# Two-layer MoE behind a Fourier mix on one core: layer two without POOL arithmetic, with later accumulations and earlier side sums

## The chip, the cores and the metric

One core of one Trainium2 chip. The metric is device microseconds of one execution, the median of several runs. Times on the trace start at the span's first instruction.

## What is computed

`x` is 2 x 3008 x 256 in float32. A Fourier transform runs over sequence and feature axis, its real part goes through two feed-forward layers of width 2048:

```python
X = np.fft.fft(np.fft.fft(x, axis=1), axis=2).real.astype(np.float32).reshape(6016, 256)
h = X @ w_in                                            # layer one
X = (np.maximum(h, 0) + alpha * np.minimum(h, 0)) @ w_out
h = X @ moe2_w_in                                       # layer two
out = (h * (1.0 / (1.0 + np.exp(-h)))) @ moe2_w_out
```

## The kernel before

The symmetry of the transform leaves half of the tokens. They are cut into six **chunks** (c = 0 to 5) of up to 512 columns. Every float32 product is done as three TensorE passes, high x high, low x high and high x low, where `high` is a rounded copy (ScalarE, ACT) and `low` is the remainder (a subtraction on VectorE, DVE, or on POOL).

**Layer one** runs in 96 steps (16 per chunk): three plus three passes into a bank, the leaky step on DVE and ACT, `gh` (ACT, L726) and `gl` (POOL, L727), then twelve passes into `pso` (L742). Into these steps the program slips side work by tables of step numbers: the Fourier stages of later chunks, the narrowing of the 64-bit weights, and for layer two `factors` (L835, L836, L840: splits of x into high and low) and `x2_sums` (L785: four subtractions per chunk, on POOL, whose result is stored to DRAM as `xf` by L789 on SP's queue).

**Layer two** works on **pairs** of 128 hidden rows, eight per chunk (p = 0 to 7). It is a fast matrix product with seven products instead of eight. Chunk 0 is done the plain way: per pair seven steps of one trio (L883, three passes) with pieces of the pair before's second product (L977) between them; two of its four lows are POOL's (`ghl`, L904). Chunks 1 to 5 follow the lists `SEQ`: one string per kind of pair, whose tokens are issued in that order. M1 to M7 are trios of the first product (L883); O1 to O7 are groups of three passes of the second (L1078), a pair late (`-1`); 7 + 7 times three is 42 passes a pair. u and m copy a bank (ACT), c adds a bank (DVE, L1090), s is the silu (ACT, L1098), T a difference of two results (L1091), h a high (ACT, L1092), l a low (L1091), E a sum on DVE. A token that ends in `g` has its subtraction on POOL instead of DVE. `sequence(c, p)` picks the string: A, B, C for the first three pairs of chunks 2 to 5, F0 to F2 for chunk 1, N in the middle, L at the end, K5 and L5 for the last two pairs of all.

Three things run beside that in chunks 1 to 4 and 2 to 5:

- **Factors of the next chunk** (`fh`, `fl`, one of each in pairs 1 to 7). `make_high` copies the high out of `raw32` into one of three spare tiles (`tail[c, "spare"][i % 3]`) and sends the previous factor to DRAM (`fdr`, L1029, SP). `make_low` writes minus the rounded value (L1037) and has POOL issue a DMA that adds the exact x onto it (L1038).
- **Ends of the chunk before** (`ending`): copies of the accumulators (L1137), then accumulations a1 to a5 as POOL DMAs into the output tile `ob` (L1129), by the table `DRAIN` behind M7 of a pair: a1, a3 in pair 2, a2 in pair 3, a4 and a5 in pair 4. a4 adds `o[:, 0, 1]` onto `o[:, 1, 1]`, and a5 then writes `o[:, 0, 1]`. Each finished quarter is written out by `write` (L1122, SP).
- **SP's queue** carries `sring` (weights of the second product), `sides` (raw32), `fdr`, the quarters of the output and, in chunk 0, the weights `y<-stash_o` and `y<-stash_i` that narrowing had put by.

POOL, SP, ACT and DVE each take their instructions in the program's order: a waiting one holds all behind it.

Of the kernel before, what the change touches and what calls it, by code (L numbers as in the profile page):

```python
# [14 lines left out]
ALU = mybir.AluOpType  # L15
# [14 lines left out]
BUFS = {"h": 2, "r": 2, "gh": 3, "gl": 2, "pb": 2, "raw": 2, "y": 2}  # L30
# [67 lines left out]
def kernel(  # L98
# [110 lines left out]
    def place_raw():  # L209
        while started and held[3] == BUFS["raw"]:  # L210
            yield EARLY
        held[3] += 1
# [55 lines left out]
    stage_s = {}  # L268

    def mixed_wout(n, y):  # L270

        a = [[y[:, m, k * P:(k + 1) * P] for k in range(2)] for m in range(2)]
        while True:
            c = now[0] // NF
            if now[0] % NF < NF - 3:
                if c not in stage_s:
                    t = spot(f"px{c - 1}", [2, 4, 2, P], F32R, "stage_s")
                    stage_s[c] = [t[:, i] for i in range(2)]
                if stage_s[c]:
                    break  # L280
            yield EARLY
        w = stage_s[c].pop(0)
        s = f32(w)[:, :, 1]
        yield AMID
        G.tensor_tensor(s[:, 0], a[0][1], a[1][1], op=ALU.add)
        G.tensor_tensor(s[:, 1], s[:, 0], a[0][0], op=ALU.subtract)
        yield EARLY
        yield AMID
        G.tensor_tensor(s[:, 2], a[0][0], a[0][1], op=ALU.subtract)
        G.tensor_tensor(s[:, 3], a[1][0], s[:, 1], op=ALU.subtract)  # L290
        active.append([store_s(n, c, w, s), EARLY])

    def store_s(n, c, w, s):
# [8 lines left out]
        stage_s[c].append(w)  # L302
# [504 lines left out]
    def slot(n):  # L807

        if n not in slots:
            if n < 4 or n > 7:  # L810
                t = spot({0: "px4", 2: "wo1_0", 8: "px3"}[n], [2, 2, 512], F32R, "ts")
# [8 lines left out]
    def place(c, j):  # L820
        return (7 * (c - 1) + 5 + j) % 8 if c else (0, 1, 2, 3, 8, 9, 4)[j]
# [200 lines left out]
    def make_high(c, i):  # L1022
        u = MAKE[i]
        t = made[c, u] = tail[c, "spare"][i % 3]
        A.activation(t[0], raw32[(7 * c + i) % 2], AF.Copy)
        while unsaved:
            v = unsaved.pop()
            for a in range(2):
                nc.sync.dma_start(fdr[v][:, a], f32(made[v][a]))  # L1029

    unsaved = []

    def make_low(c, i):
        u = MAKE[i]
        lo = made[c, u][1]
        g, s, k = SOURCE[TURN[u]]
        A.activation(lo, raw32[(7 * c + i) % 2], AF.Copy, scale=-1.0)  # L1037
        G.dma_start(f32(lo), xf[c][g][:, s, k], accum_op=ALU.add)  # L1038
        if i + 2 < 7:
            load_raw32(c, i + 2)  # L1040
        if 2 <= u < 6:
            unsaved.append((c, u))
        else:
            factor[c, TURN[u]] = made[c, u]
            split2.add((c, TURN[u]))
# [34 lines left out]
    def token(n, name, other):  # L1080
# [26 lines left out]
        elif name == "E":  # L1107
# [4 lines left out]
            else:  # L1112
                add(outbuf(c)[:, 0, 0], tail["acc"], accum[c, "O1"])
                write(c, 0, 0)
# [43 lines left out]
    def perform(n, name, other):  # L1158
# [34 lines left out]
    def start_win2():  # L1193
# [35 lines left out]
    }  # L1229
    DRAIN = {2: "a1 a3", 3: "a2", 4: "a4 a5"}  # L1230
# [29 lines left out]
    with tc.manual_schedule():  # L1260
# [181 lines left out]
        def sequence(c, p):  # L1442
# [4 lines left out]
            return "ABCNNNNL"[p] if c > 1 else "NNNNNNNL"[p]  # L1447
# [9 lines left out]
        for n, (c, p) in enumerate(pairs):  # L1457
# [110 lines left out]
```

## Time and profile before

| what | us |
|---|---|
| median of three runs (lowest, highest) | 955.98 (955.15, 958.06) |
| profiled execution | 955.43 |
| its span, first to last instruction | 953.6 |

The page gives busy time per engine; the trace gives each instruction's start, duration and, in brackets, the engine's idle time before it and what ended that. A row of the timeline may stand for several instructions (`x3`). A window's row gives the busy time of each engine in that stretch, the granted TensorE clock (1.00 is 2.4 GHz, 0.50 is 1.2 GHz) and the DMA engines' share.

### The profile page before, as it was taken

To read this page: it belongs to the slowest core of one execution; us is meant where nothing else is said; L and a number is where in the kernel's file an instruction comes from. 1 tells how busy PE (TensorE), PEld (TensorE's weight loads), DVE (VectorE), ACT (ScalarE), POOL (GpSimd) and SP (SyncE) were. 2 spreads that over 40 slices of the span, in tenths; PEclk is the share of its full clock that TensorE was granted. 3 is DMA by queue.
4 is the path that set the end of the run, shared out by engine and by line. 5 is a ranking of instruction groups with operands and counts; after the bars stand their busy time and mean duration, and the time that the engine had idled before them with its cause. 6 is when DMAs were issued, how large, how long until landed. Compare 5 with 4: busy or idle time off the path is not lost.

```text
span 953.6 us, 12772 instructions
## 1 busy us (share of the span) xinstructions
PE 923.8 (97%) x4237; PEld 767.5 (80%) x4237; DVE 757.8 (79%) x1130; ACT 697.3 (73%) x1247; POOL 529.8 (56%) x390
## 2 busy tenths in 40 slices
PE   9999999999999999999999999999899999999997
PEld 8899888888788787788897878877778778777875
DVE  4877755676787699766665689998899798899998
ACT  5787666666675576666665788898799789788775
POOL 0498868585786688999897642223223213313121
PEclk9999999999999999999999999999999999999999
DMA  9411123134333450112212267539566863964421
GB/s 340 146 45 51 48 56 75 50 86 158 132 133 126 125 169 22 48 64 78 82 51 84 73 161 198 173 103 232 154 178 160 226 178 98 243 172 130 109 78 66
DMA packets 58477, 116.83 MB, mean 123 GB/s; under 512 B 7238, under 2 KB 14508, under 8 KB 57260
## 3 DMA queue, kind: packets, MB, share of 16 engines
q1 hardware_dynamic: 50780, 102.35, 33.7%
q0 software_dynamic: 6912, 12.59, 7.8%
q10 hardware_dynamic: 720, 1.10, 0.3%
q8 instruction: 33, 0.54, 0.2%
q14 instruction: 32, 0.26, 0.1%
HBM read 77.32 MB, written 33.44 MB: 116 GB/s over the span
## 4 chain that ended last, share of the span: by engine, by line
PE 68%; issue 10%; POOL 9%; DVE 6%; DMA 4%; ACT 2%; SPq 0%; POOLq 0%; ACTq 0%; DVEq 0%
PE pso L742 21%; PE psh L883 16%; PE psh L651 11%; PE psm L1078 10%; PE pso L977 3%; POOL gl L727 2%; PE psE L1078 2%; PE psB L466 1%; DVE ghl L1091 1%; PE psW L602 1%; POOL ob L1129 1%; DVE ring L1090 1%; DVE ring L1091 1%; PE psU L1322 1%; POOL forms L1091 1%
## 5 line engine op out<-in xcount | busy, mean ns | idle before, releaser
L727 POOL TENSOR_TENSOR gl<-r,gh 128x1024 fp32r<-128x1024 f32 (+1 forms) x96 | 227.2, 2368 | 59.2 <-ACT gh L726 37.1
L883 PE MATMUL psh<-ts,wi 128*128 128x512 f32 (+1 forms) x864 | 229.8, 389 | 5.3 <-DVE ring L1090 3.1
L883 PEld LDWEIGHTS psh<-ts,wi 128*128 128x128 f32 x864 | 161.9, 189 | 41.3 <-DVE ring L1090 6.0
L742 PE MATMUL pso<-gh,wo_o 128*128 128x512 f32 (+1 forms) x768 | 191.6, 387 | 0.5 <-ACT x L759 0.5
L742 PEld LDWEIGHTS pso<-gh,wo_o 128*128 128x128 f32 x768 | 143.9, 188 | 28.3 <-ACT x L759 0.9
L651 PE MATMUL psh<-pq,wa 128*128 128x512 f32 (+1 forms) x576 | 148.5, 391 | 3.4 <-DVE h L671 3.1
L1091 DVE TENSOR_TENSOR ghl<-ring,ghl 128x512 fp32r<-128x512 f32 x185 | 139.8, 770 | 8.7 <-ACT ghl L1092 8.7
L1092 ACT ACTIVATE ghl<-ring 128x512 fp32r<-128x512 f32 x200 | 122.5, 624 | 30.2 <-DVE ring L1091 13.5
L700 DVE SCALAR_TENSOR_TENSOR psd<-h,psh 128x512 f32<-128x512 f32 (+1 forms) x96 | 65.6, 683 | 88.5 <-PE psh L651 87.8
L651 PEld LDWEIGHTS psh<-pq,wa 128*128 128x128 f32 x576 | 106.5, 188 | 26.2 <-DVE h L671 5.1
L726 ACT ACTIVATE gh<-r 128x1024 fp32r<-128x1024 f32 (+1 forms) x96 | 99.9, 1040 | 35.2 <-DVE r L711 32.9
L1091 DVE TENSOR_TENSOR ring<-ring 128x512 f32<-128x512 f32 x153 | 111.0, 726 | 13.7 <-POOL forms L1091 9.4
L701 ACT ACTIVATE r<-psh 128x512 f32<-128x512 f32 (+1 forms) x96 | 56.5, 588 | 74.4 <-DVE psd L700 58.4
L742 PE MATMUL pso<-gl,wo_o 128*128 128x512 f32 (+1 forms) x384 | 101.7, 386 | 0.1
L1078 PE MATMUL psm<-ghl,sring 128*128 128x512 f32 x360 | 96.1, 391 | 1.2 <-DVE ghl L1091 1.2
L1090 DVE TENSOR_TENSOR ring<-ring,psh 128x512 f32<-128x512 f32 x120 | 81.7, 681 | 9.9 <-ACT ring L1092 5.0
L1092 ACT ACTIVATE ring<-psh 128x512 f32<-128x512 f32 x120 | 70.7, 589 | 18.2 <-PE psh L883 18.0
L742 PEld LDWEIGHTS pso<-gl,wo_o 128*128 128x128 f32 x384 | 71.9, 188 | 14.5 <-POOL gl L727 1.1
L1098 ACT ACTIVATE ring<-ring 128x512 f32<-128x512 f32 x120 | 74.5, 624 | 11.1 <-DVE ring L1090 10.9
L711 DVE SCALAR_TENSOR_TENSOR r<-r,al,psh 128x512 f32<-128x512 f32 (+1 forms) x96 | 70.7, 736 | 14.9 <-ACT r L701 13.4
L1078 PEld LDWEIGHTS psm<-ghl,sring 128*128 128x128 f32 x360 | 67.5, 188 | 17.1 <-DVE ghl L1091 2.8
L1038 POOL DMA_DIRECT2D ts<-xf x21 | 19.4, 926 | 106.8 <-ACT ts L1037 98.4
(148 smaller groups left out, 1524.7 us busy)
## 6 DMA issues: line engine op xcount, KB each, us to landing
sring<-sdr SPq DMA_DIRECT2D x40, 512.0 KB, 4.1
raw<-in_w_in SPq DMA_DIRECT2D x16, 512.0 KB, 6.4
raw<-in_w_out SPq DMA_DIRECT2D x16, 512.0 KB, 3.6
xf<-x SPq DMA_DIRECT2D x8, 1024.0 KB
sides<-xf SPq DMA_DIRECT2D x28, 256.0 KB, 4.7
ts<-fdr SPq DMA_DIRECT2D x26, 256.0 KB, 5.5
fdr<-ts SPq DMA_DIRECT2D x24, 256.0 KB, 4.6
ts<-xf POOLq DMA_DIRECT2D x21, 256.0 KB, 5.8
```

What stands on the lines that cost most here:

```text
L651: T.matmul(bank[:, :w], wa[q][:, mm, eo, a, :], pq[c][:, 2 * eo + bb, :w], start=eo == 0 and a == bb, stop=bb == 1, skip_group_check=True)
L700: V.scalar_tensor_tensor(other[:, :w], t[:, :w], 2.0, bank[:, :w], op0=ALU.mult, op1=ALU.subtract)
L711: V.scalar_tensor_tensor(r[:, s, :w], r[:, s, :w], al[:, m:m + 1], h[:, :w], op0=ALU.mult, op1=ALU.add)
L726: A.activation(hi[:, :, :w], r[:, :, :w], AF.Copy)
L727: G.tensor_tensor(lo[:, :, :w], r[:, :, :w], f32(hi[:, :, :w]), op=ALU.subtract)
L742: T.matmul(po[c][s][k][:, :w], wo1[q][:, mm, a, k * P:(k + 1) * P], g[:, s, :w], start=m == 0 and a == 0 and g is hi, stop=m == NF - 1 and ...
L883: T.matmul(dst[:, :w], wi2[p][:, FORMS[j], a], t[:, :w], start=start and a == 0 and t is hi, stop=t is lo, skip_group_check=True)
L1078: T.matmul(dst, w, form[f][:, g], start=first and b == g == 0, stop=last and g == 1, skip_group_check=True)
L1090: add = lambda dst, a, b: V.tensor_tensor(dst, a, b, op=ALU.add)
L1091: sub = lambda dst, a, b: eng.tensor_tensor(dst, a, b, op=ALU.subtract)
L1092: copy = lambda dst, src: A.activation(dst, src, AF.Copy)
L1098: A.activation(side_of[f], x if f == "21" else side_of[f], AF.Silu)
```

## The change

- The lists of `SEQ` are new (C is dropped; the third pair is an N). None of the strings of chunks 1 to 4 has a `g` token; K5 and L5 leave three subtractions to POOL.
- `DRAIN` puts a4 into pair 4 and a5 into pair 5. Chunks before the last write their four quarters together, behind M7 of pair 6 (`LAST`).
- `make` replaces `make_high` and `make_low`; in most strings the low comes first, and a factor is stored when the high of the factor two later is made.
- `raw` has three buffers and there is a tile `more` (8 KB a partition). It holds `stage_s` in layer one and two factor slots in chunk 0; chunk 1's factors get slots of their own, all but one.
- The step tables `SUMS`, `AGAIN` and `T1` are earlier: chunk 2's sums by 16 to 19 steps, chunk 3's by 8 to 17, chunk 4's (reloaded by `again`) by 17 to 20, chunk 5's by 20 to 26, chunk 1's factors by 4 to 15.

The diff, with one of the new strings:

```diff
-BUFS = {"h": 2, "r": 2, "gh": 3, "gl": 2, "pb": 2, "raw": 2, "y": 2}
+BUFS = {"h": 2, "r": 2, "gh": 3, "gl": 2, "pb": 2, "raw": 3, "y": 2}
...
-                    t = spot(f"px{c - 1}", [2, 4, 2, P], F32R, "stage_s")
+                t = spot("more", [2, 4, 2, P], F32R, "stage_s")
...
-                t = spot({0: "px4", 2: "wo1_0", 8: "px3"}[n], [2, 2, 512], F32R, "ts")
+                t = spot({0: "px4", 2: "wo1_0", 8: "px3", 10: "more"}[n], [2, 2, 512], F32R, "ts")
...
-        return (7 * (c - 1) + 5 + j) % 8 if c else (0, 1, 2, 3, 8, 9, 4)[j]
+        return ((0, 1, 2, 3, 8, 9, 4), (5, 6, 12, 7, 10, 11, 0))[c][j]
...
+    def make(c, i, low):
+        u = MAKE[i]
+        if (c, u) not in made:
+            made[c, u] = tail[c, "spare"][i % 3]
+        hi, lo = made[c, u]
+        raw = raw32[(7 * c + i) % 2]
+        if low:
+            g, s, k = SOURCE[TURN[u]]
+            A.activation(lo, raw, AF.Copy, scale=-1.0)
+            G.dma_start(f32(lo), xf[c][g][:, s, k], accum_op=ALU.add)
+        else:
+            A.activation(hi, raw, AF.Copy)
+            if i > 1 and 2 <= MAKE[i - 2] < 6:
+                for a in range(2):
+                    nc.sync.dma_start(fdr[c, MAKE[i - 2]][:, a], f32(made[c, MAKE[i - 2]][a]))
+        if (c, u, not low) in halfway:
+            if i + 2 < 7:
+                load_raw32(c, i + 2)
...
-            write(c, 1, 0)
+            write(c, 1, 0, c == NC - 1)
...
-        "N": ("M1 s22-1 h21-1 E-2 s12-1 M2 h22-1 O1-1 m1 fh l21-1 M6 T1-1 l22-1 O3-1 hT1-1 c11 T3-1 M5 fl lT1-1 "
-               "u2 hT3-1 M7 s11 O5-1 u3 T2-1 lT3-1 T4-1 O7-1 M4 hT2-1 c22 M3 h11 hT4-1 s21 lT2-1 lT4-1 c12 O6-1 "
-               "O2-1 O4-1 l11g "),
+        "N": ("M1 s12-1 h21-1 O3-1 E-2 T1-1 m1 l21-1 fl hT1-1 M2 M6 T3-1 O1-1 c11 M5 hT3-1 T2-1 lT1-1 u2 M7 "
+               "hT2-1 lT3-1 O5-1 s11 u3 T4-1 c22 h11 lT2-1 hT4-1 s22 O7-1 M4 M3 O6-1 s21 O2-1 h22 lT4-1 l11 O4-1 "
+               "c12 fh l22 "),
...
-    DRAIN = {2: "a1 a3", 3: "a2", 4: "a4 a5"}
+    DRAIN = {2: "a1 a3", 3: "a2", 4: "a4", 5: "a5"}
+    LAST = 6
...
-    SUMS = {2: (69, 72, 75, 78), 3: (81, 86, 88, 89), 5: (126, 132, 134, 139)}
-    AGAIN = 111, 4, (115, 118, 120, 124)
-    T1 = 40, 42, 46, 47, 48, 49, 50, 51, 53, 54, 55
+    SUMS = {2: (50, 56, 57, 60), 3: (66, 69, 78, 81), 5: (106, 108, 111, 113)}
+    AGAIN = 90, 4, (96, 98, 103, 105)
+    T1 = 28, 30, 31, 33, 36, 38, 43, 44, 47, 49, 51
...
+                    if p == LAST:
+                        for i in range(4):
+                            write(c - 1, i // 2, i % 2)
```

Three places show how the instructions stand. First POOL in pairs 2 to 6 of chunk 2; `ts<-xf` is a factor's low, `ob<-` are the accumulations, `forms` the low of a result that PE needs. Before:

```order
L1038 DMA ts<-xf_1_69 128x512 x2
L1129 DMA ob<-ob 128x512
L1091 TENSOR_TENSOR forms<-ring,forms 128x512
L1038 DMA ts<-xf_1_69 128x512
L1129 DMA ob<-ob 128x512
L1129 DMA ob<-t_98 128x512
L1091 TENSOR_TENSOR forms<-ring,forms 128x512
L1038 DMA ts<-xf_0_68 128x512
```

and after:

```order
L1030 DMA ts<-xf_1_69 128x512
L1129 DMA ob<-ob 128x512
L1030 DMA ts<-xf_1_69 128x512
L1129 DMA ob<-ob 128x512
L1030 DMA ts<-xf_0_68 128x512
L1129 DMA ob<-t_98 128x512
L1030 DMA ts<-xf_0_68 128x512 x2
```

The `forms` rows are gone from POOL, and `ob<-t_98` (a5) no longer stands right behind the accumulation whose source it overwrites (a4).

Second, POOL in pairs 0 to 2 of chunk 0; `ghl` are the lows of chunk 0's results, `wi` and `wAo` weights, `x` the side sums. Before:

```order
L904 TENSOR_TENSOR ghl<-ring,ghl 128x448
L382 TENSOR_TENSOR wi_5_4420<-t_98,wi_5_4420 128x4x128
L904 TENSOR_TENSOR ghl<-ring,ghl 128x448
L324 TENSOR_TENSOR wAo_4170<-y_4500,wAo_4170 128x2x256
L324 TENSOR_TENSOR wAo_4529<-y_4502,wAo_4529 128x2x256
L904 TENSOR_TENSOR ghl<-ring,ghl 128x448
```

and after:

```order
L902 TENSOR_TENSOR ghl<-ring,ghl 128x448
L783 TENSOR_TENSOR x_4147<-x_4147 128x512
L380 TENSOR_TENSOR wi_5_4422<-t_98,wi_5_4422 128x4x128
L783 TENSOR_TENSOR x_4147<-x_4147 128x512
L783 TENSOR_TENSOR x_4445<-x_4445 128x512
L902 TENSOR_TENSOR ghl<-ring,ghl 128x448
L783 TENSOR_TENSOR x_4445<-x_4445 128x512
L322 TENSOR_TENSOR wAo_4171<-y_4505,wAo_4171 128x2x256
L322 TENSOR_TENSOR wAo_4536<-y_4507,wAo_4536 128x2x256
L902 TENSOR_TENSOR ghl<-ring,ghl 128x448
```

Four side sums now stand between the lows of pair 0's end and pair 1's end.

Third, SP in pairs 4 to 6 of chunk 2. Before:

```order
L1020 DMA sides<-xf_0_68 128x512
L1122 DMA out_dram<-ob 128x512
L1014 DMA sring<-sdr_2818 128x1024
L1029 DMA fdr_4_80<-ts 128x512 x2
L1020 DMA sides<-xf_0_68 128x512
L1122 DMA out_dram<-ob 128x512 x2
L1014 DMA sring<-sdr_3061 128x1024
L1029 DMA fdr_5_81<-ts 128x512 x2
```

and after:

```order
L1012 DMA sring<-sdr_3064 128x1024
L1035 DMA fdr_4_80<-ts 128x512 x2
L1018 DMA sides<-xf_0_68 128x512
L1012 DMA sring<-sdr_3209 128x1024
L1122 DMA out_dram<-ob 128x512 x4
L1035 DMA fdr_5_81<-ts 128x512 x2
```

The stores of factors and the loads no longer stand behind single quarters of the output; the last store of a factor stands behind all four.

## Rows read from the trace of the kernel before

**Rows 1.** The page, part 1: engine, busy us, share of the span, instructions.

```profile
PE 923.8 (97%) x4237; PEld 767.5 (80%) x4237; DVE 757.8 (79%) x1130; ACT 697.3 (73%) x1247; POOL 529.8 (56%) x390
```

**Rows 2.** Windows by chunk of layer two: length, busy (instructions) by engine, clock, DMA.

```profile
459.50:536.50 77.00, 74.67 (x361) 67.45 (x360) 50.56 (x74) 47.95 (x91) 65.72 (x60) 1.00 0.26 88
536.50:617.10 80.60, 77.46 (x340) 63.09 (x339) 71.26 (x104) 69.29 (x132) 26.48 (x23) 1.00 0.56 151
617.10:699.50 82.40, 78.79 (x338) 63.85 (x337) 72.89 (x113) 69.90 (x132) 22.95 (x22) 0.98 0.66 176
699.50:781.00 81.50, 78.75 (x337) 63.81 (x336) 72.82 (x113) 69.67 (x132) 22.86 (x22) 0.98 0.66 177
781.00:862.10 81.10, 78.03 (x337) 62.48 (x337) 73.26 (x113) 69.71 (x133) 22.92 (x22) 1.00 0.66 179
862.10:953.60 91.50, 84.01 (x358) 65.94 (x356) 84.22 (x127) 68.84 (x127) 22.11 (x18) 0.99 0.32 86
```

**Rows 3.** Timeline of PE: start, us; the first trio of pairs 3 to 6, chunk 2.

```profile
646.44 0.84 PE L883 MATMUL psh<-spare,wi 128*128 128x512 f32 x3
...
655.96 0.84 PE L883 MATMUL psh<-spare,wi 128*128 128x512 f32 x3
...
666.41 0.84 PE L883 MATMUL psh<-spare,wi 128*128 128x512 f32 x3
...
680.34 0.84 PE L883 MATMUL psh<-spare,wi 128*128 128x512 f32 x3
```

**Rows 4.** Waits of PE, whole span: us in total, times, longest.

```profile
PE psm L1078 <- POOL forms L1091: 5.9, 3, 2.5
```

**Rows 5.** Timeline around the longest of these waits: POOL and PE.

```profile
661.16 1.20 POOL L1129 DMA_DIRECT2D ob<-ob  x1
...
668.70 0.87 POOL L1129 DMA_DIRECT2D ob<-t  x1 [6.34 <-PE psm L1078]
...
670.92 0.64 PE L1078 MATMUL psm<-forms,wAo 128*128 128x512 f32 x1 [2.54 <-POOL forms L1091]
```

**Rows 6.** Windows: the stretch after that wait, columns as in rows 2.

```profile
671.10:674.50 3.40, 3.40 (x9) 2.62 (x10) 3.40 (x6) 2.77 (x5) 0.88 (x1) 0.50 0.65 139
```

**Rows 7.** Timeline, pair 4 of chunk 2: ACT and PE.

```profile
658.61 0.63 ACT L1025 ACTIVATE ts<-sides 128x512 fp32r<-128x512 f32 x1 [1.14 <-DMA fdr<-ts]
...
660.81 0.97 PE L883 MATMUL psh<-ts,wi 128*128 128x512 f32 x3 [0.61 <-ACT ring L1092]
```

**Rows 8.** Timeline, pair 0 of chunk 3: DVE beside POOL and alone.

```profile
699.51 1.59 POOL L1091 TENSOR_TENSOR forms<-ring,forms 128x512 fp32r<-128x512 f32 x1
699.61 2.05 DVE L1091 TENSOR_TENSOR ring<-ring 128x512 f32<-128x512 f32 x1
...
703.99 1.28 DVE L1091 TENSOR_TENSOR ghl<-ring,ghl 128x512 fp32r<-128x512 f32 x2
```

**Rows 9.** Groups by line: busy, mean ns of one, idle before and its releasers.

```profile
L1091 POOL TENSOR_TENSOR forms<-ring,forms 128x512 fp32r<-128x512 f32 x29 | 41.5, 1431 | 58.3 <-ACT forms L1092 58.3
...
L785 POOL TENSOR_TENSOR x<-x 128x512 f32<-128x512 f32 x16 | 21.8, 1367 | 0.1
```

**Rows 10.** Timeline of chunk 0, pairs 1, 2, 5: POOL's lows, PE.

```profile
476.56 1.16 POOL L904 TENSOR_TENSOR ghl<-ring,ghl 128x448 fp32r<-128x448 f32 x1 [2.31 <-ACT ghl L899]
...
480.22 1.53 POOL L904 TENSOR_TENSOR ghl<-ring,ghl 128x448 fp32r<-128x448 f32 x1
...
481.69 0.98 PE L977 MATMUL pso<-ghl,wAo 128*128 128x448 f32 x4
...
507.68 1.25 ACT L323 ACTIVATE wAo<-y 128x512 fp32r<-128x512 f32 x2 [3.67 <-DMA y<-stash_o]
...
512.44 0.47 PE L977 MATMUL pso<-ghl,wAo 128*128 128x448 f32 x1 [1.29 <-POOL ghl L904]
```

**Rows 11.** Waits of PE's weight loads, whole span, columns as in rows 4.

```profile
PEld pso L742 <- POOL gl L727: 1.1, 3, 0.5
```

**Rows 12.** The page, part 6: DMA issues, KB each, median us to landing.

```profile
fdr<-ts SPq DMA_DIRECT2D x24, 256.0 KB, 4.6
```

More of the change, by code (lines that the diff above doesn't have):

```diff
@@ L209, in place_raw @@
     def place_raw():
-        while started and held[3] == BUFS["raw"]:
+        while started and held[3] == 2:
             yield EARLY
@@ L266, in keep_back @@
         return narrow(src, finish, own_y=True)
-    stage_s = {}
+    stage_s = []
     def mixed_wout(n, y):
@@ L273, in mixed_wout @@
         while True:
-            c = now[0] // NF
-            if now[0] % NF < NF - 3:
-                if c not in stage_s:
-                    t = spot(f"px{c - 1}", [2, 4, 2, P], F32R, "stage_s")
-                    stage_s[c] = [t[:, i] for i in range(2)]
-                if stage_s[c]:
-                    break
+            if not stage_s:
+                t = spot("more", [2, 4, 2, P], F32R, "stage_s")
+                stage_s.append([t[:, i] for i in range(2)])
+            if stage_s[0]:
+                break
             yield EARLY
-        w = stage_s[c].pop(0)
+        w = stage_s[0].pop(0)
         s = f32(w)[:, :, 1]
@@ L290, in mixed_wout, with store_s @@
         G.tensor_tensor(s[:, 3], a[1][0], s[:, 1], op=ALU.subtract)
-        active.append([store_s(n, c, w, s), EARLY])
-    def store_s(n, c, w, s):
+        active.append([store_s(n, w, s), EARLY])
+    def store_s(n, w, s):
         yield EARLY
@@ L301, in store_s @@
         nc.sync.dma_start(sdr[n].rearrange("p i a f -> p (i a f)"), f32(w).rearrange("p i a f -> p (i a f)"))
-        stage_s[c].append(w)
+        stage_s[0].append(w)
     def bring_back(key, finish, lead):
@@ L809, in slot @@
         if n not in slots:
-            if n < 4 or n > 7:
-                t = spot({0: "px4", 2: "wo1_0", 8: "px3"}[n], [2, 2, 512], F32R, "ts")
+            if n < 4 or 7 < n < 12:
+                t = spot({0: "px4", 2: "wo1_0", 8: "px3", 10: "more"}[n], [2, 2, 512], F32R, "ts")
                 slots[n], slots[n + 1] = ([t[:, i, j] for j in range(2)] for i in range(2))
@@ L1020, in load_raw32 @@
         nc.sync.dma_start(raw32[(7 * c + i) % 2], xf[c][g][:, s, k])
-    def make_high(c, i):
+    def make(c, i, low):
         u = MAKE[i]
[L1024 to L1042, printed above, removed]
-        else:
-            factor[c, TURN[u]] = made[c, u]
-            split2.add((c, TURN[u]))
+        if (c, u) not in made:
[6 more added lines that the diff above has]
+            G.dma_start(f32(lo), xf[c][g][:, s, k], accum_op=ALU.add)
+        else:
+            A.activation(hi, raw, AF.Copy)
[5 more added lines that the diff above has]
+                load_raw32(c, i + 2)
+            if u < 2 or u == 6:
+                factor[c, TURN[u]] = made[c, u]
+                split2.add((c, TURN[u]))
+        halfway.add((c, u, low))
+    halfway = set()
     def refill(c, v):
@@ L1113, in token @@
                 add(outbuf(c)[:, 0, 0], tail["acc"], accum[c, "O1"])
-                write(c, 0, 0)
+                write(c, 0, 0, c == NC - 1)
     def outbuf(c):
@@ L1119, in outbuf, with write @@
         return po[c, 3]
-    def write(c, s, k):
-        (A if c == NC - 1 and s == k else nc.sync).dma_start(out[k, :, s, c], po[c, 3][:, s, k])
+    def write(c, s, k, now=True):
+        if now:
+            (A if c == NC - 1 and s == k else nc.sync).dma_start(out[k, :, s, c], po[c, 3][:, s, k])
     def ending(c, name, other):
@@ L1149, in ending @@
             add(o[:, 1, 1], o[:, 1, 1], o[:, 0, 1])
-            write(c, 1, 1)
+            write(c, 1, 1, c == NC - 1)
         elif name == "a5":
             add(o[:, 0, 1], o[:, 0, 1], rest4)
-            write(c, 0, 1)
+            write(c, 0, 1, c == NC - 1)
     copied, performed = set(), set()
@@ L1168, in perform @@
         elif name == "fh":
-            make_high(c + 1, p - 1)
+            make(c + 1, p - 1, False)
         elif name == "fl":
-            make_low(c + 1, p - 1)
+            make(c + 1, p - 1, True)
         else:
@@ L1446, in sequence @@
                 return f"{'KL'[p - 6]}5"
-            return "ABCNNNNL"[p] if c > 1 else "NNNNNNNL"[p]
+            return "ABNNNNNL"[p] if c > 1 else "NNNNNNNL"[p]
         def ahead(step):
```

49 rows, old and new, of the table SEQ are left out of this document.

## The prediction

> **What bounds the kernel now.** I began with the page: TensorE (PE) is busy for 97% of the span [rows 1]. A PE that is nearly always busy can only give back what it still loses, so the rest of the reading looks for PE's lost time and nothing else. Second came the windows by chunk: layer two takes 494 of the 953.6 us [rows 2]. Third the timeline of PE, by the first trio of each pair: pair 3 of chunk 2 takes 655.96 - 646.44 = 9.52 us [rows 3], and it holds 42 passes, 0.227 us each. I found no shorter pair of that kind, so I take 9.52 as the floor. Eight of them are 76.2 us. The windows then tell the loss of each chunk [rows 2]: chunk 1 80.6 (0.2 of it are three more passes), so 4.2 lost; chunk 2 82.4, 6.2 lost; chunk 3 81.5, 5.3; chunk 4 81.1, 4.9; chunk 5 with the end 91.5 against 7 x 9.52 + 63 x 0.227 = 80.9, so 10.6, of which the larger part is the drain of the outputs behind the last pass. About 20.6 us of loss stand in chunks 1 to 4: that is the purse.
>
> **Where it is lost.** Pair 5 of chunk 2 takes 680.34 - 666.41 = 13.93, that is 4.4 over the floor, and pair 4 takes 10.45, 0.9 over [rows 3]. The waits name pair 5's cause: PE waits for POOL's `forms` three times, 5.9 us together, once in each of chunks 2 to 4 [rows 4]. POOL itself was not busy: it issued a4 at 661.16, then stood before a5 until 668.70, since a5 overwrites what a4's DMA still reads, and the low that PE needs lay queued behind it [rows 5]. After that wait the granted clock is 0.50, the 1.2 GHz level, from 671.1 to 674.5 [rows 6], another 3.4 x 0.5 = 1.7 us; the same falls on chunk 3 but not on chunk 4, as their clocks of 0.98 and 1.00 show [rows 2]. Pair 4: ACT stood 1.14 us before a factor, because the spare tile's earlier content was still on its way to DRAM, and PE then lacked a bank copy [rows 7]. Pair 0: a POOL subtraction of 1.59 us held a DVE instruction, which took 2.05 instead of the 0.6 to 0.7 that it takes alone [rows 8].
>
> **The change, part by part.**
>
> *POOL's subtractions go to DVE.* In layer two's listed pairs POOL has 29 `forms` lows of 1.43 us [rows 9], and 22 more of its kind; three stay. So 48 go to DVE. Two DVE instructions in a row end 1.28 us after the first began and take 0.68 each, so the second starts 0.60 after the first [rows 8]: 48 x 0.60 = 29 us of DVE work, spread over 40 pairs. What covers it: a pair has 15 DVE instructions after the change (7 lows, 4 differences, 3 adds, 1 sum), 15 x 0.60 = 9.0 against 9.52. If that cover is gone, each 0.04 us of pitch costs 0.6 us a pair. DVE also gains, as the stretch of about 1.4 us that one POOL subtraction can hold it is gone.
>
> *A pair a5 later, POOL free.* With nothing for PE on POOL's queue, the wait before a5 delays only the next factor's DMA, which the next chunk needs. The three pair-5 stalls go: in chunk 2 4.4 us. What is next late there? In N the low of 22 is issued last in the pair and O3 asks for it 0.7 us into the next; I followed the rest of the string with the durations above and found 0.5 us or more in hand at each trio, and about 1 us at T1's, T2's and T3's lows.
>
> *Stores of factors.* They no longer queue behind single quarters of the output. A store lands 4.6 us after issue in the median [rows 12]; in pairs 1 to 6 it has over 10 us until its tile is rewritten. One is tight: the last store stands behind the four quarters in pair 6, and ACT rewrites its tile some 2.5 us into pair 7. I cost that at nothing (the stores are ready about 1 us into pair 6, so 4.6 us and the four issues leave some 2 us); if it fails, the price is pair 4's of today, 0.9 us a chunk.
>
> *Sum for chunks 1 to 4:* I keep 0.5 us of loss in chunk 1 (its first pairs share ACT and POOL with chunk 0's end) and 0.3 in the others, so 20.6 - 1.4 = 19.2 gained; bounds 11 (the pair-5 stalls alone, 5.9 of waiting and 3.4 of clock, and half of the 4.2 in chunk 1) and 20.6.
>
> *Chunk 5 and the end.* Its 10.6 hold the stall of pair 0 once more (as in chunk 3 [rows 8]), and stalls in the last two pairs. K5 has 18 DVE instructions (10.8 us), which run into L5; I take 2.5 gained, bounds 0 and 4. The drain stays.
>
> *Chunk 0: the sums now stand among its lows.* Today POOL starts pair 1's first low at 476.56 after 2.3 us idle, and its second at 480.22, ending 481.75; PE uses that one in the group of four from 481.69, at its third pass, 482.3 [rows 10]. So there is 0.5 us in hand. After the change eight subtractions of 1.37 us [rows 9] come between the last layer-one low and this place or just behind it. Two come before, and they eat what three subtractions taken out of steps 86 to 89 give back. The three between pair 0's second low and pair 1's first take 4.1, less the 2.3 idle: 1.8 late. One more after it: 3.2 late in all, less 0.5: PE stands 2.7 us in pair 2. A weight load queued behind the sums' store on SP may be late too, up to 2 us for ACT. In return the store in front of `y<-stash_o` is gone, for which ACT stood 3.67 us and PE 1.29 and about 1 more in pair 5 [rows 10], 2.8 us with what the restart costs. Price: 2.7 to 4.5, I take 3.3, and half of the 1.7 that a clock drop would cost, since PE's wait is as long as the one of rows 5; net 1.3 lost, bounds 3.4 lost and 2.8 gained.
>
> *Layer one.* Sums move to steps 50 to 66, where POOL has idle time, and leave steps 72 to 89, where POOL runs behind and PE's weight loads wait for `gl` 1.1 us [rows 11]. I take 0.9 gained, bounds -1 (a DVE instruction held by POOL's longer runs) and +1.1.
>
> *Total:* 19.2 + 2.5 - 1.3 + 0.9 = 21.3. The profiled execution, 955.43 with 953.6 of span, becomes 934.1; the median of the runs lies 0.55 higher, so **934.5**.
>
> **A rule that speaks against it.** Two DVE lows in a row start 0.60 us apart here [rows 8]. The Trainium skill, "VectorE: DVE Perf Modes", section "The DRAIN you can't avoid", says that after each DVE operation the pipe is emptied before the next one starts, and only adds that one which is not held starts earlier. By the first half alone a pair would need 15 x 0.68 = 10.2 us and DVE would set the pace; by the rows it is 9.0, and the sum goes by those.
>
> **Rivals.**
>
> 1. *DVE becomes the bound (slower).* Mechanism: the 15 DVE instructions of an N pair, each dependent on a fresh ACT result, come at their whole duration, 0.68, and not at 0.60. That is 10.25 us a pair, 0.73 over the floor, in some 35 pairs: +25.6, against the 21.3 gained: 960. This is what the rule above would make of the time. It decides from a pitch of 9.52 / 15 = 0.635. Against it: chunk 2 today runs 113 DVE instructions in 82.4 us 14 a pair, with undisturbed pairs of 9.52 among them [rows 2, 3], and the change adds one to a pair. For it: DVE is then at 95%. Chance 0.08.
> 2. *No gain.* Pairs A and K5 with 17 and 18 DVE instructions, pair 7's ACT behind the last store and chunk 0's backlog each bring a new stall with a clock drop behind it: (2.5 + 1.7) in four chunks and 4.5 in chunk 0 take the 21 back: 956. Against it: each has slack by the count above. Chance 0.06.
> 3. *Half of the gain in the new places.* Only two of those come: the last store late in three chunks with a dropped clock in some (0.9 to 2.6 each, 6 together) and chunk 0 at its upper bound (2.1 more): 942.5, with a spread from 939 to 947. Chance 0.17.
> 4. *More than forecast.* POOL enters chunk 0 with less of a backlog, the 2.7 us stall does not come, and the end is clean: -2.8 - 1.3 - 1.5 = 929. Chance 0.11.
> 5. The forecast, with its own bounds 930 to 939: 0.58.
>
> **How the numbers follow.** Time 934.5. Cases 3, 4 and 5 hold 0.86; cut at 927 below (case 4 with layer one's upper bound) and 945 above (most of case 3), some 0.17 is left out. This kernel can be told from no change from about 0.3% on, 2.9 us, so "within" is 953.1 to 958.8: that is case 2, 0.06. Faster 0.86, slower 0.08 (case 1).
>
> **What would show it.** Right: no wait of PE for POOL's `forms` at all; eight pairs of 9.5 to 9.6 in chunks 2 to 4, windows of 76.5 to 77; clock 1.00 there; DVE instructions near 0.68, none over 1 us before K5. POOL's busy time of 23 us in chunk 2 falls to about 12, the DMAs alone. The chunk-0 step: PE waits for `ghl` on POOL in pair 2, near 482 on today's clock, and no wait for `y<-stash_o` in pair 5. Wrong: pairs of 10 us with DVE gapless (rival 1); ACT waiting for `fdr` in pair 7 (rival 3); PE waits in A or K5 for DVE.

## The result, and the profile after

| what | before | after |
|---|---|---|
| median of four runs, us (lowest, highest) | 956.37 (955.15, 958.06) | 932.48 (931.49, 935.99) |
| ratio after / before, 95% interval | | 0.9756 (0.9725, 0.9786) |
| profiled execution, us | 955.43 | 931.89 |
| its span, us | 953.6 | 930.1 |

The forecast was 934.5 with a range of 927 to 945; the change gained 23.9 us by the medians. Line numbers of the changed kernel are two lower in its upper part (the trio is L881, the group L1077, low and difference on DVE L1090, chunk 0's low L902).

The page of after, part 1 (engine, busy us, share of the span, instructions) answers to [rows 1]: PE is busy 8 us less in a span that is 23.5 us shorter, and POOL has lost 67 us.

```profile
PE 915.7 (98%) x4237; PEld 768.2 (83%) x4237; DVE 764.7 (82%) x1178; ACT 701.8 (75%) x1247; POOL 463.2 (50%) x342
```

The windows by chunk, columns as in [rows 2]:

```profile
456.34:535.08 78.74, 75.40 (x361) 67.35 (x360) 52.28 (x76) 50.58 (x93) 67.22 (x62) 1.00 0.21 72
535.08:611.62 76.54, 76.54 (x340) 63.61 (x339) 70.22 (x115) 68.48 (x127) 6.23 (x8) 1.00 0.59 156
611.62:687.87 76.25, 76.25 (x338) 63.05 (x336) 74.20 (x122) 70.21 (x132) 10.53 (x12) 1.00 0.72 190
687.87:764.11 76.24, 76.24 (x338) 63.04 (x336) 74.20 (x122) 70.20 (x132) 10.55 (x12) 1.00 0.72 190
764.11:840.35 76.24, 76.24 (x337) 63.05 (x336) 74.19 (x122) 70.20 (x132) 10.55 (x12) 1.00 0.72 190
840.35:930.10 89.75, 83.54 (x358) 66.05 (x356) 84.46 (x135) 69.86 (x127) 8.51 (x8) 0.99 0.32 91
```

In chunks 1 to 4 PE's busy time equals the length of the window: no gap is left. Chunk 0 alone has become longer (78.74 against 77.00). The whole, term by term, each from the difference of two windows (layer one from the start of chunk 0):

| term | forecast, gained us | in the profile |
|---|---|---|
| layer one | 0.9 | 3.16 |
| chunk 0 | -1.3 | -1.74 |
| chunk 1 | 3.7 | 4.06 |
| chunks 2, 3, 4 | 5.9, 5.0, 4.6 | 6.15, 5.26, 4.86 |
| chunk 5 and the end | 2.5 | 1.75 |
| sum | 21.3 | 23.5 |

Timeline of PE, first trio of pairs 3 to 6 of chunk 2, against [rows 3]: 9.52 us from row to row, pair 5 too.

```profile
640.20 0.84 PE L881 MATMUL psh<-spare,wi 128*128 128x512 f32 x3
...
649.72 0.84 PE L881 MATMUL psh<-spare,wi 128*128 128x512 f32 x3
...
659.24 0.84 PE L881 MATMUL psh<-spare,wi 128*128 128x512 f32 x3
...
668.76 0.84 PE L881 MATMUL psh<-spare,wi 128*128 128x512 f32 x3
```

Timeline of POOL in pairs 4 and 5, against [rows 5]: a4, a factor's low, a5. In chunks 2 to 4 POOL stands before a factor's DMA until ACT has written the tile, and nowhere else; in chunk 5, which has no factors to make, it still stands 5.45 us before a4 and 2.81 before a5, with nothing for PE behind them.

```profile
652.55 1.22 POOL L1129 DMA_DIRECT2D ob<-ob  x1
661.68 0.88 POOL L1030 DMA_DIRECT2D ts<-xf  x1 [7.91 <-ACT ts L1029]
662.22 1.23 POOL L1129 DMA_DIRECT2D ob<-t  x1
```

The waits of PE over the whole span (us in total, times, longest); no row for `forms` is left [rows 4]:

```profile
PE pso L975 <- POOL ghl L902: 3.3, 1, 3.3
PE psh L649 <- DVE h L669: 2.2, 4, 0.8
PE psB L464 <- DMA ur<-tmid: 1.6, 1, 1.6
PE idle L1271 <- POOL zero L1262: 1.1, 1, 1.1
PE psm L1077 <- DVE ghl L1090: 0.2, 1, 0.2
```

The first of them is the forecast stall of chunk 0. Timeline of POOL and PE there (rows of other instructions left out), against [rows 10]: three `x` (side sums) with a weight among them, the first low, another sum, two weights, and only then the second low. POOL has no gap there. PE stands before it for 3.28 us.

```profile
470.94 1.67 POOL L783 TENSOR_TENSOR x<-x 128x512 f32<-128x512 f32 x1
472.58 1.30 POOL L380 TENSOR_TENSOR wi<-t,wi 128x512 fp32r<-128x512 f32 x1
473.82 2.56 POOL L783 TENSOR_TENSOR x<-x 128x512 f32<-128x512 f32 x2
476.33 1.16 POOL L902 TENSOR_TENSOR ghl<-ring,ghl 128x448 fp32r<-128x448 f32 x1
477.45 1.68 POOL L783 TENSOR_TENSOR x<-x 128x512 f32<-128x512 f32 x1
479.10 2.87 POOL L322 TENSOR_TENSOR wAo<-y,wAo 128x512 fp32r<-128x512 f32 x2
481.93 1.13 POOL L902 TENSOR_TENSOR ghl<-ring,ghl 128x448 fp32r<-128x448 f32 x1
...
483.11 0.47 PE L975 MATMUL pso<-ghl,wAo 128*128 128x448 f32 x1 [3.28 <-POOL ghl L902]
```

### The profile page after: what moved, and what is told of

The parts are those of the page before. It is cut to its first block, busy times and chain, and to the rows that moved or that the text cites. A ratio compares the mean times of both kernels' runs of the same rounds, so it can differ in the third digit from the quotient of the medians.

```text
span 930.1 us, 12673 instructions
## 1 busy us (share of the span) xinstructions
PE 915.7 (98%) x4237; PEld 768.2 (83%) x4237; DVE 764.7 (82%) x1178; ACT 701.8 (75%) x1247; POOL 463.2 (50%) x342
## 4 chain that ended last, share of the span: by engine, by line
PE 90%; DVE 5%; POOL 1%; issue 1%; ACT 1%; DMA 1%; SPq 0%; ACTq 0%; DVEq 0%; POOLq 0%
PE pso L740 25%; PE psh L881 23%; PE psm L1077 17%; PE psh L649 13%; PE pso L975 4%; PE psE L1077 2%; PE psB L464 2%; PE psU L1320 2%; PE psW L600 2%; DMA ur<-tmid 1%; DVE ring L1090 1%; DVE r L709 1%; DVE ghl L1090 1%; DVE psd L698 0%; POOL x L783 0%
## 5 line engine op out<-in xcount | busy, mean ns | idle before, releaser
L881 PE MATMUL psh<-ts,wi 128*128 128x512 f32 (+1 forms) x864 | 227.1, 386 | 0.0
L881 PEld LDWEIGHTS psh<-ts,wi 128*128 128x128 f32 x864 | 161.6, 188 | 32.8 <-ACT ring L1091 1.7
L740 PEld LDWEIGHTS pso<-gh,wo_o 128*128 128x128 f32 x768 | 144.0, 188 | 27.5
L1090 DVE TENSOR_TENSOR ghl<-ring,ghl 128x512 fp32r<-128x512 f32 x197 | 130.7, 690 | 0.1
L1090 DVE TENSOR_TENSOR ring<-ring 128x512 f32<-128x512 f32 x160 | 110.6, 691 | 0.4 <-ACT ring L1097 0.2
L1077 PE MATMUL psm<-ghl,sring 128*128 128x512 f32 x360 | 95.7, 390 | 0.2 <-DVE ghl L1090 0.2
L1077 PEld LDWEIGHTS psm<-ghl,sring 128*128 128x128 f32 x360 | 67.5, 188 | 15.3 <-DVE ghl L1090 1.1
```

The source lines that it names most:

```text
L740: T.matmul(po[c][s][k][:, :w], wo1[q][:, mm, a, k * P:(k + 1) * P], g[:, s, :w], start=m == 0 and a == 0 and g is hi, stop=m == NF - 1 and ...
L881: T.matmul(dst[:, :w], wi2[p][:, FORMS[j], a], t[:, :w], start=start and a == 0 and t is hi, stop=t is lo, skip_group_check=True)
L1077: T.matmul(dst, w, form[f][:, g], start=first and b == g == 0, stop=last and g == 1, skip_group_check=True)
L1090: sub = lambda dst, a, b: eng.tensor_tensor(dst, a, b, op=ALU.subtract)
```

## Experiments

The theory is that of the prediction: in chunks 1 to 4 the time came from two causes, POOL standing before a5 with PE's low behind it, and POOL's subtractions holding DVE; the moved sums give a little in layer one and take a little in chunk 0. Each run was compared with the kernel before on the same chip, whose medians there were 955.2 to 955.8.

**One part alone: a5 a pair later.**

```diff
 (kernel before)
-    DRAIN = {2: "a1 a3", 3: "a2", 4: "a4 a5"}
+    DRAIN = {2: "a1 a3", 3: "a2", 4: "a4", 5: "a5"}
```

> The kernel before with one edit: a5 a pair after a4; POOL keeps all its subtractions. Theory (PE's low stood behind a5, which stood behind a4's DMA): the three pair-5 stalls go, 4.4 + 3.6 + 3.0 = 11.0 us, pairs 0 and 4 of each chunk keep their 0.7 and 0.9: 945.4, and no wait of PE for POOL's forms in chunks 2 to 4. Rival (POOL's subtractions themselves are late, whatever stands before them): the stall moves to pair 6, 954 to 957.

Measured: 944.11, ratio 0.988 (0.9859, 0.9901), 11.5 us less. Pair 5 of chunks 2 to 4 takes 9.52 to 9.55. Timeline of POOL in pair 5, with the subtraction still there: a5 goes out at once, and the low follows.

```profile
669.31 1.20 POOL L1129 DMA_DIRECT2D ob<-t  x1
671.91 1.39 POOL L1091 TENSOR_TENSOR forms<-ring,forms 128x512 fp32r<-128x512 f32 x1 [1.40 <-ACT forms L1092]
```

So this one line of a table carries about half of the gain, with all of POOL's arithmetic in place.

**The other part alone: no subtractions on POOL.**

```diff
 (kernel before; the same for each g token of A, B, C, F0, F1, F2)
-               "O2-1 O4-1 l11g "),
+               "O2-1 O4-1 l11 "),
```

> The kernel before with one edit: the subtractions that the strings of chunks 1 to 4 (and of the first six pairs of chunk 5) leave to POOL go to DVE; order, a4 and a5 as they were. Theory: POOL still stands 6 us before a5 but nothing of PE's is behind it, so pair 5 takes 9.52 (11.0 gained); pair 0's DVE instruction of 2 us is gone (4 x 0.75 and up to 1.5 in chunk 1); pair 4's 0.9 stays, since that is ACT behind a store: 956.4 - 11.0 - 3.0 - 1.5 = 941, 938 to 943. Rival (DVE at 15 instructions a pair becomes the bound): pairs of 10 us, 960.

Measured: 940.29, ratio 0.9842 (0.982, 0.9864). POOL still stands 6.52 us before a5, and pair 5 takes 9.52 all the same. POOL's timeline names a4's DMA as what ended that wait; [rows 5] named PE there, so that the prediction's reading, that a5 waits for a4's DMA, is shown by this row.

```profile
665.44 0.88 POOL L1129 DMA_DIRECT2D ob<-t  x1 [6.52 <-DMA ob<-ob]
```

What was left in pair 4 is a factor's spare tile that is still being stored [rows 7], in the waits of ACT:

```profile
ACT ts L1025 <- DMA fdr<-ts: 4.1, 3, 1.8
```

Either edit removes the pair-5 stalls. The second also shortens pair 0 of chunks 2 to 4, from 10.27 to 10.31 us down to 9.67 to 9.69, but pair 1 then takes 10.05 instead of 9.52: there PE's weight loads wait 0.35 and 0.44 us for DVE. So with the old strings nearly all of pair 0's loss comes back a pair later; with the new strings pairs 0 and 1 take 9.52 and 9.54. The two gains (11.5 and 15.3) overlap and don't add up. ACT's wait, 0.7 to 1.5 us of PE in each of three chunks here, is not in the waits of ACT of after. The new order of stores is the likely reason, but no run has it alone, nor the new strings alone.

**The changed kernel with a5 back behind a4.**

```diff
-    DRAIN = {2: "a1 a3", 3: "a2", 4: "a4", 5: "a5"}
+    DRAIN = {2: "a1 a3", 3: "a2", 4: "a4 a5"}
```

> The changed kernel with a5 back behind a4 in pair 4. Theory (with nothing for PE on POOL's queue the wait before a5 is free): POOL stands some 6 us in pair 4 of chunks 2 to 5, PE loses nothing, 932.5 within 0.5. Rival (the factor's low that stands behind a5 is late for its store, its raw32 or its spare tile): ACT waits in pair 5 to 7, 1 to 3 us a chunk, 936 to 942.

Measured: 932.03, ratio 0.9761 (0.9733, 0.979). POOL waits again and PE loses nothing by it; pairs 4 to 7 of chunks 2 to 4 take 9.52 to 9.59.

```profile
659.20 0.87 POOL L1129 DMA_DIRECT2D ob<-t  x1 [5.43 <-DMA ob<-ob]
```

In the changed kernel, then, the later a5 is worth nothing.

**A subtraction back on POOL.**

```diff
-               "... lT4-1 l11 O4-1 c12 fh l22 "
+               "... lT4-1 l11g O4-1 c12 fh l22 "
```

> The changed kernel with one low of each N pair (that of 11, 23 pairs) back on POOL. Theory (a POOL subtraction beside DVE holds one DVE instruction up to 1.4 us longer, rows 8; DVE has some 0.5 us a pair to spare and 0.6 more without this low): 0 to 0.3 lost a pair, 932.5 to 939. Rival (only a5's place cost time, POOL's arithmetic does not): 932.0 to 932.5, pairs of 9.52.

Measured: 937.88, ratio 0.9814 (0.9793, 0.9834): 5.4 us over the changed kernel, and the 23 N pairs take 9.77 to 9.80, 23 x 0.26 = 6.0. Timeline of POOL, DVE and PE in one of them: the two DVE lows take 2.40 us together beside POOL's 1.29, where [rows 8] has 1.28 for two alone.

```profile
646.63 1.29 POOL L1090 TENSOR_TENSOR forms<-ring,forms 128x512 fp32r<-128x512 f32 x1 [2.09 <-ACT forms L1091]
646.67 2.40 DVE L1090 TENSOR_TENSOR ghl<-ring,ghl 128x512 fp32r<-128x512 f32 x2
...
647.95 1.07 PE L1077 MATMUL psm<-ghl,sring 128*128 128x512 f32 x3
```

The weight loads of the group behind wait for them, by the waits of PE's weight loads:

```profile
PEld psm L1077 <- DVE ghl L1090: 10.0, 25, 0.6
```

One DVE instruction less in a pair did not pay for it. The Trainium skill, "SBUF — State Buffer", section "SBUF: two separate sides", says that a GpSimd instruction that reads SBUF and a DVE instruction with two SBUF inputs exclude each other for the whole instruction. The trace agrees: POOL's instruction had begun 0.04 us before the two lows, and they ended 1.1 us later than alone, a little less than its 1.29.

**How far DVE is from being the bound.**

```diff
 (in token(), behind the low; second run: f in ("22", "T2"))
+            if c and (c < NC - 1 or p < 6) and f in ("22",):
+                sub(form[f][:, 1], side_of[f], f32(form[f][:, 0]))
```

> The changed kernel with one DVE subtraction more in each of 38 pairs of layer two (the low of 22 is formed twice). Theory (DVE starts an instruction every 0.60 us and has 15 in a pair of 9.52): 16 x 0.60 = 9.6, so 0.08 a pair at most: 932.5 to 935.5. Rival (each waits for a fresh result, 0.64 a piece and more): 10.2 a pair, 958.

> As before, with two more (the lows of 22 and T2 formed twice), 17 a pair. Theory (0.60 us each): 10.2 a pair, 0.68 x 38 = 26 us more, 958, and DVE without a gap. Rival (DVE had room beyond the count, its pitch being smaller in a full queue, or its late results cost nothing): 933 to 940.

Measured: 944.43 with one more, ratio 0.989 (0.9871, 0.9909), and 972.11 with two more, ratio 1.0178 (1.0159, 1.0198). Both lie above what was expected. One pair of each follows as a window (columns as above; an instruction that a window's edge cuts is counted too). The changed kernel, with 15 DVE instructions in the pair's list:

```profile
640.20:649.72 9.52, 9.52 (x43) 7.88 (x42) 9.20 (x16) 8.65 (x17) 1.76 (x2) 1.00 0.81 194
```

With 16:

```profile
671.98:681.77 9.79, 9.79 (x43) 7.80 (x42) 9.76 (x17) 8.70 (x17) 0.87 (x1) 1.00 0.91 270
```

With 17:

```profile
659.56:670.09 10.53, 10.36 (x43) 7.66 (x43) 10.46 (x18) 8.71 (x17) 1.75 (x2) 1.00 0.70 174
```

DVE is busy for 9.20 of 9.52, 9.76 of 9.79, 10.46 of 10.53. An instruction that finds its inputs ready starts 0.60 us after the one ahead. The repeated low does not: it writes the tile that its twin has just written and waits for the twin's end, so it starts 0.72 us after it. Timeline of DVE in the pair with 16; the low and its twin take 1.41 us together, where [rows 8] has 1.28 for two lows that don't depend on each other:

```profile
679.66 0.68 DVE L1090 TENSOR_TENSOR forms<-ring,forms 128x512 fp32r<-128x512 f32 x1
680.26 0.68 DVE L1089 TENSOR_TENSOR ring<-ring,psh 128x512 f32<-128x512 f32 x1
680.86 1.41 DVE L1090 TENSOR_TENSOR forms<-ring,forms 128x512 fp32r<-128x512 f32 x2
682.18 0.68 DVE L1089 TENSOR_TENSOR sides<-sides,psE 128x512 f32<-128x512 f32 x1
```

The starts add up to the pairs: one add starts 0.65 us after the one ahead, the repeated lows 0.72, the other 14 instructions 0.602, which makes 9.80 and 10.52. So 0.12 us of each repeated low is this experiment's own price, 38 x 0.12 = 4.6 us of the first run and 9.1 of the second, about half or more of what they lie above the expectations. An instruction more that waited for nothing would make the pair 9.68 (an estimate from these starts), 0.16 over the 9.52 of PE and not 0.27. The changed kernel has 9.52 - 15 x 0.602 = 0.49 us a pair to spare, in two places where DVE waits for PE and for ACT: less than one instruction. The first one too many costs 0.27 a pair here, and the next 0.74.

**The step tables.** All three as before, then T1 alone, in the changed kernel:

```diff
-    SUMS = {2: (50, 56, 57, 60), 3: (66, 69, 78, 81), 5: (106, 108, 111, 113)}
-    AGAIN = 90, 4, (96, 98, 103, 105)
-    T1 = 28, 30, 31, 33, 36, 38, 43, 44, 47, 49, 51
+    SUMS = {2: (69, 72, 75, 78), 3: (81, 86, 88, 89), 5: (126, 132, 134, 139)}
+    AGAIN = 111, 4, (115, 118, 120, 124)
+    T1 = 40, 42, 46, 47, 48, 49, 50, 51, 53, 54, 55
```

> The changed kernel with the three step tables of the side sums (SUMS, AGAIN, T1) as before. Theory: chunk 0's wait of 3.3 us in pair 2 goes and the one of 2.8 for y<-stash_o in pair 5 comes back; in layer one the block of 2.05 at step 70 and about 1.0 of late gl at steps 77 to 82 come back, the new 1.1 at step 67 goes, and the 1.2 at steps 47 and 48 stay gone, since they are not the tables' doing but that of the tile more: 932.5 - 3.3 + 2.8 + 3.05 - 1.1 = 934. Rival (the tables are worth all of layer one's gain): 459.5 at the start of chunk 0 again, 935.2. Rival (they are worth nothing there): 932.

> The changed kernel with the table T1 alone as before (chunk 1's factors split 4 to 15 steps later). Theory (those splits then stand on ACT at the border of chunks 0 and 1): pair 0 of chunk 1 loses 2 us to ACT, as with all three tables: 934.5. Rival (that loss came from the late sums): 932.5.

Measured: 933.75, ratio 0.9771 (0.9743, 0.9799), and 934.38, ratio 0.9767 (0.9751, 0.9783). Both times are close to the theories' 934 and 934.5, by luck: the terms differ (below). Against 932.48 the intervals overlap, so that the tables are worth anything at all in sum isn't shown by the times, and the places say more. The windows of chunks 0 and 1 with all three old tables:

```profile
457.59:534.30 76.71, 74.38 (x361) 67.22 (x359) 50.59 (x74) 47.79 (x90) 65.70 (x60) 1.00 0.26 88
534.30:612.85 78.55, 76.92 (x340) 63.64 (x340) 72.24 (x117) 70.66 (x132) 11.22 (x11) 1.00 0.55 150
```

Against after, layer one is 1.25 longer (1.95 was expected), chunk 0 2.0 shorter (0.5 was expected) and chunk 1 2.0 longer. The last was not expected in that run (it was in the one of T1). With T1 alone the profile is 2.7 us longer than after: 1.45 in chunk 1, and 1.6 in chunk 0, where the clock fell behind the same stall (last section), which is not T1's doing as far as the runs show. The row of chunk 1's loss with T1 alone, from the timeline of PE in pair 0 of chunk 1, which takes 11.29 instead of 9.79: ACT, still splitting chunk 1's factors, is late with a copy of a bank.

```profile
539.84 0.97 PE L881 MATMUL psh<-ts,wi 128*128 128x512 f32 x3 [1.23 <-ACT ring L1091]
```

In layer one the block of step 70 (PE 2.05 us behind a DVE instruction L241, which lasted 4.82 beside two POOL instructions in the kernel before) is there with the old tables, and gone after. But it is gone too in the run without POOL's subtractions, whose layer one is that of the kernel before, so that it is no sure mark of the tables. The moved sums bring a like block of their own at step 67:

```profile
343.09 1.77 POOL L296 TENSOR_TENSOR stage_s<-stage_s 128x512 fp32r<-128x512 f32 x1
343.63 1.51 DVE L241 TENSOR_SCALAR y<-y 128x512 int32<-128x512 int32 x1
...
346.45 1.78 PE L649 MATMUL psh<-pq,wa 128*128 128x512 f32 x6 [0.70 <-DVE h L669]
```

**Chunk 0's stall.** First the sums of chunk 5 later, two ways (i1, i2); then one of POOL's two lows of a pair of chunk 0 on DVE (i3); then both (i4).

```diff
 (i1 and i2; i4 has i2's steps and the second edit)
-    SUMS = {..., 5: (106, 108, 111, 113)}
+    SUMS = {..., 5: (113, 115, 118, 120)}      i2: 5: (122, 125, 129, 132)
 (i3 and i4, in item())
-                    low(c, p, i, g, G)
+                    low(c, p, i, g, V if i == 1 else G)
```

> The changed kernel with chunk 5's four side sums at steps 113 to 120 instead of 106 to 113. Theory (chunk 0's wait of 3.3 us is POOL's backlog, and two sums of 1.3 and 1.7 us stand in front of that low): the wait falls to some 0.4, and the sums that stand in pairs 2 and 3 instead cost up to 2 there, since POOL is busy 9.1 of 9.3 us in pair 3: 930, 929 to 932. Rival (the wait is the DMA that feeds the weights ahead of it on POOL): 932.5.

> The same with steps 122 to 132, where POOL idles 0.8 to 3.7 us a pair. Theory: the 3.3 us wait falls to some 0.4 and nothing comes in its place, 929.4; if the passes of chunk 0 keep their shorter pitch of 0.203 us without a wait ahead of them, another 1.1: 928.3. Rival (the sums' store on SP makes y<-stash_o late, as in the kernel before): ACT waits in pair 5 or 6, PE 2.8, 932.

> The changed kernel; in chunk 0 the second of POOL's two lows of each pair (that of c22, the one PE waited for) goes to DVE. Theory: the 3.3 us wait goes, and POOL's backlog shrinks by 1.15 us a pair: chunk 0 in 75.5 instead of 78.7, 929.2, and 928.1 if the passes keep the pitch of 0.203. Rival (DVE now stands before ACT's high in every pair, and its adds make PE's banks late, 0.1 to 0.3 a pair): 930 to 931.

> The same, and chunk 5's side sums at steps 122 to 132. Theory (with that low on DVE the sums stand in nobody's way, wherever they are): as i3 within 0.5. Rival (the first low of a pair, still on POOL, was late too): 0.5 to 1 below i3. Rival (the sums come among chunk 1's splits): 0.7 above it.

Measured: 930.27 with the sums at 113, ratio 0.9744 (0.9726, 0.9763); 930.94 at 122, 0.9749 (0.9731, 0.9766); 931.54 with the low on DVE, 0.9737 (0.9721, 0.9752); 928.34 with both, 0.9712 (0.9698, 0.9725). Moving the sums cuts PE's wait in pair 2 from 3.28 us to 0.69 and 0.88 (0.4 was expected). New waits of PE for POOL come behind it: 1.02 and 0.50 in pairs 4 and 5 with the sums at 113, 0.94 in pair 5 with those at 122. At 122 ACT waits for `y<-stash_o` again, 3.07 us in pair 6, as the rival said, but PE loses 0.25 by it and not 2.8. Moving the low shifts the stall instead of removing it, against the theory: PE runs through pair 2 and stands in pair 3, before the first low, which is still POOL's. PE's wait in chunk 0 with the low moved:

```profile
PE pso L975 <- POOL ghl L902: 2.5, 1, 2.5
```

And the window of chunk 0 with both edits:

```profile
456.66:531.21 74.55, 74.13 (x362) 67.45 (x360) 57.05 (x83) 50.43 (x93) 59.48 (x54) 1.00 0.22 76
```

So the stall was a backlog of POOL, and neither the sums nor the low alone were it. With both gone PE waits for no low of POOL there, and chunk 0 takes 74.55, less than in either kernel. The sums are not free at 122: ACT waits 3.32 us for `y<-stash_o` in pair 6, which takes 9.81, and pair 0 of chunk 1 takes 10.25 instead of the 9.72 that it takes with the low alone.

The version is 27.5 us below the kernel before and 3.2 below the one with the low alone, where the theory said within 0.5; its interval just touches that of the changed kernel. In the profiled executions most of this distance is the clock: the one with the low alone holds two stretches of some 3.4 us at 1.2 GHz, one in layer one and one behind the stall, about 2 x 1.7 us, and the one with both has none before the drain at the end. In chunk 0 the two profiles differ by 3.6, of which the clock is 1.7.

## Why the prediction was right, point by point

- **Where the time is lost.** The purse of 20.6 in chunks 1 to 4 was right, and so was its emptying: 20.3 came back, 19.2 were forecast. The 0.5 and 0.3 us kept back as loss were too much; 0.1 to 0.2 a chunk is left. That the whole came within 2.2 us of the sum is partly luck: chunks 1 to 4 and layer one gave 1.1 and 2.3 more than forecast, chunk 0 and the end 0.4 and 0.75 less.
- **POOL's subtractions to DVE.** The step held: DVE instructions take 0.69 us on average in chunks 2 to 4 and none there takes over 0.7. Rival 1 didn't come: an instruction whose inputs are ready starts 0.60 after the one ahead, and the two runs with more on DVE show the whole duration, 0.72 from start to start, only where an instruction waits for the DVE instruction just ahead. The rule of the Trainium skill, "VectorE: DVE Perf Modes", section "The DRAIN you can't avoid", taken by its first half alone, would have given 10.2 us a pair; the trace stays with the rows. The room of 0.52 us a pair is 0.49 by the starts. What the step is worth by itself isn't shown: with the old strings DVE is late in pair 1 instead of pair 0.
- **a5 a pair later, POOL free.** Two reasons were given for one stall, and the runs show that removing either is enough. The first alone gave 11.5; in the presence of the second it gives nothing. That the lower bound was 11 is no hit: it counted 9.3 for these stalls (5.9 of waiting, 3.4 of clock) and half of chunk 1's loss, which the run left alone, while pair 5 by itself gave 11.1.
- **Stores of factors.** Right: costed at nothing, and no wait of ACT for `fdr` is left, in pair 4 or in pair 7, though a store now lands after 6.4 us in the median, not 4.6 [rows 12].
- **Chunk 1.** The sum was right (4.06 against 3.7), its cause half wrong. For the 4.2 lost the prediction named no cause but POOL's subtractions, and for the 0.5 kept back ACT and POOL shared with chunk 0's end. With the subtractions gone and nothing else, pair 0 still takes 11.39; with T1 late alone, 11.29. So some 1.5 of the gain is the earlier split of chunk 1's factors, a term that the prediction didn't have; the subtractions are in pairs 1 and 2.
- **Chunk 0.** The stall stands where it was forecast, in pair 2, before POOL's second low, at 3.28 us against 2.7 to 4.5; it began at 479.8, which is 23.5 us into the chunk against the 23 that "near 482" meant on the clock of before. The wait for `y<-stash_o` is gone, and the 2.8 counted for it is what pair 5 loses with the old tables (11.88 against 9.12). The drop of the clock, taken by half, didn't come in this profile, but in two of the six kernels that have this stall; passes at 0.207 us instead of 0.203 cost five pairs 0.9 us, where they cost the kernel before 0.4 (below).
- **Layer one.** The mis-sized term: 0.9 forecast, 3.16 in the profile. 1.0 is the late `gl` of steps 77 to 82 [rows 11], as forecast. 2.05 is the block at step 70, a term that the prediction didn't have; 1.1 went to the new one at step 67. 0.8 is near step 48, where ACT waited 2.7 us for `sdr<-stage_s`, a tile that `more` replaced; this wait is in the two runs built on the kernel before and in none built on the changed one. 0.6 more stands some 10 us earlier, where ACT waited 1.0 us for `pb<-rd`: it is missing in the two runs built on the kernel before and there in the changed kernel with one DVE subtraction more, so it is not the change's. In three profiles of the same layer one (before, and the two runs built on it) chunk 0 starts at 459.50, 458.25 and 457.78, and the last holds a stretch of 3.45 us at 1.2 GHz besides, some 1.7 us. Much of the 3.16 may be chance, the block at step 70 too, which one of these two runs doesn't have; only the 1.0, which every run with the old tables of sums has, and the 0.8, which every run without `more` has, are in none of the others.
- **Chunk 5 and the end.** 1.75 of 2.5. K5 loses 0.45 instead of 1.35, but L5, from its first pass to PE's last, lasts as long as before: 16.6 against 16.4.

## What to carry over

A queue that issues DMAs and does arithmetic fails by its order: one accumulation that waits for another holds whatever stands behind it, and either of two edits, a pair between them or nothing urgent behind, is enough; test each alone before paying for both. When work moves to an engine, count its instructions by the pitch from start to start, and give an instruction that waits for the one just ahead its whole duration: here 95% by the count left room for less than one instruction. A backlog of an in-order queue doesn't belong to one instruction; taking away the late one makes the next late, so move as much work as the backlog is long.

## What was not expected of the hardware

- **The same stall, two clocks.** Six kernels here have the wait of 3.28 to 3.32 us in pair 2 of chunk 0. In four the granted clock stays at 1.00 (2.4 GHz) behind it; in two it falls to the 1.2 GHz level, with a4 and a5 together for 3.5 us behind the wait, with the old T1 for 6.9 us, from 481.8, still in the wait, to 488.7. The pair takes 14.23 and 15.32 us instead of 12.7. The length of the wait doesn't decide it: with the low of chunk 0 on DVE the clock falls behind a wait of 2.54 us. What does stays open. The window behind the wait, in after:

```profile
483.11:486.51 3.40, 3.40 (x16) 3.11 (x17) 1.66 (x3) 1.48 (x3) 3.24 (x4) 1.00 0.00 1
```

With a4 and a5 together:

```profile
482.70:486.10 3.40, 3.39 (x9) 3.03 (x10) 0.62 (x1) 1.10 (x2) 3.24 (x4) 0.52 0.00 0
```

With the old T1:

```profile
482.80:486.20 3.40, 3.37 (x9) 3.04 (x10) 0.62 (x1) 1.10 (x2) 3.24 (x4) 0.50 0.00 0
```

- **Two pitches at one clock.** Chunk 0's passes of 448 columns start 0.203 us apart on average in undisturbed pairs (9.12 us for 45), or 0.207 (9.30), both at a granted clock of 1.00. A stretch of 9.30 begins behind a stall and lasts for pairs on end: pairs 3 to 7 in after, 6 and 7 in the kernel before, 3 and 4 with the sums at 122; behind the same stall the five other kernels run at 9.12. What sets it stays open; it costs 0.18 us a pair.
- **An engine held more than once.** In the kernel before, one DVE L241 (0.43 us in the median) lasted 4.82 us, from 354.76, while POOL ended one instruction and ran the next three of 1.28, 2.38 and 0.45. That POOL held it is inferred from the neighbours; if so, waiting through the first did not give it the turn before the second.
